# A one-core transformer block: a new instruction order whose model knows that VectorE and GpSimd block each other, layer norm in small groups, reciprocals as Ln and Exp

## The chip, the cores and the metric

The kernel runs on one core of one Trainium2 chip. The metric is the device time of one launch in microseconds (us). The kernel before took 233.0 us (median of 3 runs, 232.33 to 233.59). Its output was right against the reference.

## The reference, cut to what matters

One token block of 2048 rows and 512 columns goes through a modulated layer norm, linear attention with 32 heads, a second modulated layer norm and a gated feed-forward of width 1376. In the attention, queries and keys become features by two softmaxes over 16 values each (of the projection and of its negative).

```python
mod = silu(c) @ w_mod                      # shifts sa, sb; scales ca, cb; gates ga, gb
h = layernorm(x) * (1 + ca) + sa
q, k, v = split(h @ wqkv)                  # 32 heads of 16
phi_q = [softmax(q w_phi), softmax(-q w_phi)]
phi_k = [softmax(k w_phi), softmax(-k w_phi)]
kv = phi_k^T v;  z = sum(phi_k)
o = (phi_q kv) / (phi_q z + 1e-6)
x = x + ga * (o @ wo)
h = layernorm(x) * (1 + cb) + sb
x = x + gb * ((sigmoid(h @ w_gate) * (h @ w_up)) @ w_down)
```

## The kernel before

The kernel is a graph of tasks. Each task has the engines that may do it with a duration for each, a due time and an earliest time. When the kernel is built, a list scheduler plays the graph through and writes every engine's queue in the resulting order. In the traces each engine works its queue in that order, so a task that waits stops everything behind it (run e11 shows it: two sums start only when 12.39 us of scaling ahead of them on GpSimd are done).

```python
# Graph.order(), cut: the ready task with the earliest due time takes the free engine with the shortest duration
engs = [e for e in t.alts if free_at[e] <= now + 1e-9]
...
e = min(engs, key=lambda e: t.alts[e])
```

Sixteen tiles of 128 rows go through the "K stage": layer norm 1, K and V projections (the feature weights are folded into the K and Q weights first), exp, sum, reciprocal, product, and the kv matmuls. Layer norm 1 works in groups of four tiles. The first two groups are transposed on TensorE, the others by DMA:

```python
for g in range(4):
    ...
    def f_rs(e, sl=sl):                                   # rstd of four tiles, on GpSimd
        pool.tensor_scalar(ve1[:, sl], mv1[:, sl, 1], 1e-5, None, op0=ALU.add)
        pool.tensor_tensor(rs1[:, sl], ve1[:, sl], mhalf[:, sl], op=ALU.pow)
    # nmr1 = -mean * rstd, the bias of the normalisation on ScalarE or GpSimd:
    dve.scalar_tensor_tensor(nmr[:, 0, sl], mv1[:, sl, 0], -1.0, rs1[:, sl], ...)
...
G.add(f"e{t}.{a}", {"ACT": 1.12 * w}, f_e, ...)           # exp of k and of -k
G.add(f"n{t}.{a}", {"DVE": 0.08 + 1.13 * w}, f_n, ...)    # ks = sum over 16
G.add(f"r{t}.{a}", {"DVE": 0.06 + 0.5 * w}, lambda e, ...: dve.reciprocal(ks, ks), ...)
G.add(f"phi{t}.{a}", {"POOL": 0.05 + 1.9 * w} ..., f_p)   # phi = e * ks
```

After kv come, in units of one tile and later of two, the division of the attention, the output projection, layer norm 2, and the gate and up matmuls of the feed-forward:

```python
act.copy(smS[:, 0:nt], sm[:, 0:nt, 0:128])                # PSUM to SBUF
def f_small(...):
    dve.tensor_tensor(m[:, 0:nt], smS[:, 0:nt, 0:64], smS[:, 0:nt, 64:128], op=ALU.mult)
    dve.tensor_tensor(den[:, 0:nt], m[:, 0:nt, 0:32], m[:, 0:nt, 32:64], op=ALU.add)
    dve.reciprocal(den[:, 0:nt], den[:, 0:nt])
    dve.tensor_tensor(cc[:, 0:nt], smS[:, 0:nt, 64:128]..., den[:, 0:nt]..., op=ALU.mult)
```

GpSimd also scales wo by ga (4 pieces, shared with VectorE) and wd by gb (11 pieces, "wd scaling"), the latter soon after kv. The silu at the start uses Tanh, as does the sigmoid of the feed-forward.

## Time and profile before

| what | before | how to read it |
|---|---|---|
| time | 233.0 us | median of 3 runs; the profiled run has a span of 230.8 |
| TensorE work at full rate | 197.0 us | worked out in the prediction |
| steady K matmuls from | 15.3 us | what lies before is the start |
| last kv matmul ends | 69.7 us | end of the K stage |
| first gate matmul | 90.2 us | after it TensorE has one hole, of 0.50 us |
| ScalarE busy | 103.1 us (45%) | VectorE 75%, GpSimd 36% |
| table loads on ScalarE | 1 | see below |

The prediction shows the main lines.

A table load is an instruction on ScalarE's own queue of 1.283 us. In the K stage (15.3 to 69.7 us) ScalarE is busy for 42.90 of 54.40 us and VectorE for 49.07.

### The profile page before, as it was taken

The numbers are of one execution on the slowest core, as the hardware profiler recorded it, in microseconds if no ns is written. First come the engines' busy times: TensorE is split into PE (matmuls) and PEld (weight loads), VectorE is DVE, ScalarE is ACT, GpSimd is POOL, SyncE is SP. The second block draws the span as 40 slices with busy tenths as digits, with TensorE's granted clock in tenths as the row PEclk, the third lists the DMA queues.
The fourth block names the chain that finished last, engine by engine and source line by source line (L and its number), as shares of the span: only waits on it lengthen the run. The fifth ranks groups of instructions, "written<-read, shape, count | busy, mean of one in ns | idle before, by whom it ended". The sixth has DMA issues, their size and how long they took to land.

```text
span 230.8 us, 4164 instructions
## 1 busy us (share of the span) xinstructions
PE 206.3 (89%) x1526; PEld 117.6 (51%) x1526; DVE 172.3 (75%) x355; ACT 103.1 (45%) x207; POOL 82.4 (36%) x91
## 2 busy tenths in 40 slices
PE   0588798899889769999999999999999999999990
PEld 0563555355445457876877544445454444444430
DVE  0689998759997998978999974958677988432430
ACT  2578685879785546443453233252321432322100
POOL 6405599679499725323200620110430300000000
PEclk9999999999999967999999999999999999999998
DMA  6974836059900002113222220132202061000011
GB/s 173 366 285 91 313 141 97 0 103 378 341 6 3 0 0 48 24 27 71 45 68 57 46 59 3 26 68 68 48 0 68 0 104 47 12 1 23 27 59 43
DMA packets 30333, 19.27 MB, mean 83 GB/s; under 512 B 22257, under 2 KB 27746, under 8 KB 30306
## 3 DMA queue, kind: packets, MB, share of 16 engines
q1 hardware_dynamic: 30272, 18.91, 29.1%
q8 instruction: 14, 0.23, 0.4%
q0 software_dynamic: 32, 0.02, 0.2%
q14 instruction: 13, 0.11, 0.2%
q10 hardware_dynamic: 2, 0.00, 0.0%
HBM read 11.58 MB, written 2.10 MB: 59 GB/s over the span
## 4 chain that ended last, share of the span: by engine, by line
PE 60%; ACT 0%; DVE 0%; issue 0%
PE u_ps L471 17%; PE g_ps L471 17%; PE y_ps L491 16%; PE a_ps L396 6%; PE num L363 2%; PE sm L338 1%; ACT eT L772 0%; PE q_ps L767 0%; DVE ot L500 0%; PE tp_x L443 0%; PE bnd L526 0%
## 5 line engine op out<-in xcount | busy, mean ns | idle before, releaser
L475 ACT ACTIVATE tg<-g_ps 128x512 bf16<-128x512 f32 (+5 forms) x66 | 29.5, 454 | 70.1 <-PE g_ps L471 59.1
L480 DVE SCALAR_TENSOR_TENSOR wmod_sb<-tg,u_ps 128x512 bf16<-128x512 bf16 (+5 forms) x66 | 32.3, 503 | 25.8 <-PE u_ps L471 21.7
L491 PE MATMUL y_ps<-wd_sb,wmod_sb 128*128 128x512 bf16 (+1 forms) x176 | 44.4, 379 | 0.0
L725 POOL TENSOR_TENSOR phi<-e,ks 128x1024 bf16<-128x1024 bf16 (+1 forms) x15 | 28.3, 1898 | 11.3 <-DVE ks L730 5.0
L471 PEld LDWEIGHTS <-wg_sb 128*128 128x128 bf16 (+1 forms) x264 | 23.5, 100 | 17.3 <-DVE wT_sb L450 0.5
L471 PEld LDWEIGHTS <-wu_sb 128*128 128x128 bf16 (+1 forms) x264 | 23.6, 100 | 16.4 <-issue 0.8
L387 POOL TENSOR_TENSOR o<-u 128x512 bf16<-128x512 f32 x14 | 17.9, 1287 | 35.6 <-DVE u L369 33.9
L471 PE MATMUL g_ps<-wT_sb,wg_sb 128*128 128x512 bf16 (+3 forms) x132 | 27.0, 326 | 0.0
L471 PE MATMUL u_ps<-wT_sb,wu_sb 128*128 128x512 bf16 (+3 forms) x132 | 26.8, 326 | 0.0
L491 PEld LDWEIGHTS <-wmod_sb 128*128 128x128 bf16 (+1 forms) x176 | 16.9, 98 | 17.5
L471 PE MATMUL u_ps<-wqk_sb,wu_sb 128*128 128x128 bf16 (+5 forms) x132 | 22.1, 290 | 0.5 <-ACT eT L772 0.5
L471 PE MATMUL g_ps<-wqk_sb,wg_sb 128*128 128x128 bf16 (+5 forms) x132 | 22.2, 290 | 0.0
L369 DVE TENSOR_TENSOR u<-num,cc 128x512 f32<-128x512 f32 (+1 forms) x32 | 20.6, 679 | 1.2 <-PE num L363 1.1
L722 DVE TENSOR_REDUCE ks<-e 128x64 f32<-128x1024 bf16 (+1 forms) x18 | 19.0, 1064 | 2.2 <-ACT e L719 2.2
L719 ACT ACTIVATE e<-k_ps 128x512 bf16<-128x512 f32 x32 | 17.2, 611 | 5.0 <-PE k_ps L706 3.4
L772 ACT ACTIVATE eT<-q_ps 128x512 bf16<-128x512 f32 x32 | 16.7, 621 | 3.7 <-PE q_ps L767 2.6
L706 PE MATMUL k_ps<-wqk_f,h1T 128*128 128x512 bf16 x64 | 16.2, 380 | 1.5 <-ACT h1T L691 0.8
L396 PE MATMUL a_ps<-wo_sb,oT 128*128 128x512 bf16 x64 | 16.1, 394 | 0.7 <-ACT eT L772 0.7
L412 POOL TENSOR_SCALAR ve<-mv 128x2 f32<-128x2 f32 (+1 forms) x9 | 2.0, 225 | 41.1 <-DVE mv L406 39.9
L710 PE MATMUL v_ps<-wv_sb,h1T 128*128 128x512 bf16 x64 | 16.1, 379 | 0.1
L767 PE MATMUL q_ps<-h1T,wqk_f 128*128 128x512 bf16 x64 | 15.5, 379 | 0.0
L500 DVE TENSOR_TENSOR ot<-y_ps,x 128x512 bf16<-128x512 f32 x16 | 11.0, 686 | 5.9 <-PE y_ps L491 5.8
(110 smaller groups left out, 280.8 us busy)
## 6 DMA issues: line engine op xcount, KB each, us to landing
x_sb<-in_A_x_dram SPq DMA_DIRECT2D x4, 512.0 KB, 9.9
wmod_sb<-in_w_mod_dram SPq DMA_DIRECT2D x1, 2048.0 KB, 8.0
out_dram<-ot SPq DMA_DIRECT2D x16, 128.0 KB, 1.8
wg_sb<-in_B_w_gate_dram SPq DMA_DIRECT2D x1, 1376.0 KB, 7.5
wu_sb<-in_B_w_up_dram SPq DMA_DIRECT2D x1, 1376.0 KB
wd_sb<-in_B_w_down_dram SPq DMA_DIRECT2D x1, 1280.0 KB, 13.5
wqk_sb<-in_A_wqkv_dram SPq DMA_DIRECT2D x2, 512.0 KB, 5.9
wmod_sb<-in_w_mod_dram SPq DMA_DIRECT2D x1, 1024.0 KB, 8.4
```

The costliest lines, as they stand in the source:

```text
L369: dve.tensor_tensor(u[:], ps[:].rearrange("p (h d) -> p h d", d=DH), cc[:, q, s, :].unsqueeze(2).to_broadcast([P, H, DH]), op=ALU.mult)
L387: G.add(f"o{t}", {"POOL": 1.3}, lambda e, ub=ub, o=o: pool.tensor_tensor(o[:], ub[0][:].rearrange("p h d -> p (h d)"), ub[1][:].rearrange( ...
L396: pe.matmul(ap_[:], lhsT=oT[:, j, :], rhs=wo_sb[:, j, :], start=(j == 0), stop=(j == KT - 1))
L471: pe.matmul(ps[:fsz, 0:n], lhsT=w[:, j, ft * P:ft * P + fsz], rhs=h[:, j, 0:n], start=(j == 0), stop=(j == KT - 1))
L475: G.add(f"tg{k}.{ft}", {"ACT": 0.15 + n * 0.00088}, lambda e, tg=tg, g_ps=g_ps, fsz=fsz, n=n: act.activation(tg[:fsz, 0:n], g_ps[:fsz, 0:n ...
L480: dve.scalar_tensor_tensor(hm_all[:fsz, hm[k].slot, ft, 0:n], tg[:fsz, 0:n], 1.0, u_ps[:fsz, 0:n], op0=ALU.add, op1=ALU.mult)
L491: pe.matmul(y[:], lhsT=hm_all[:fsz, hm[k].slot, ft, tl * P:(tl + 1) * P], rhs=wd_sb[:fsz, ft, :], start=(ft == 0), stop=(ft == FT - 1))
L706: pe.matmul(kp[:], lhsT=h1T[:, j, t * P:(t + 1) * P], rhs=wqk_f[:, j, D:2 * D], start=(j == 0), stop=(j == KT - 1))
L719: act.activation(ee[:, s].rearrange("p h j -> p (h j)"), kp[:], ACT.Exp, scale=1.0 - 2.0 * s)
L722: dve.tensor_reduce(ks[:, a:b], ee[:, a:b], axis=AX.X, op=ALU.add)
L725: engine(e).tensor_tensor(ph[:].rearrange("p (s h j) -> p s h j", s=2, j=DH)[:, a:b], ee[:, a:b], ks[:, a:b].unsqueeze(3).to_broadcast([P, ...
L772: act.activation(eT[cq][:, s * 4 + blk, :], qp[:], ACT.Exp, scale=1.0 - 2.0 * s)
```

## The change

Its intent is to take out the places where VectorE and GpSimd block each other and to fill TensorE's holes. By "lock" I mean below what the traces show: beside a GpSimd operation some VectorE operations take several times as long (in the kernel before, den, with two SBUF inputs, took 1.05 us for 128x32 under the wd scaling and 0.22 for 128x64 after it). The scheduler's model gets this lock, better durations and searched due times: in the code, tasks marked with `port` don't run on the two engines at one time. Layer norm 1 works in groups of one and two tiles, all transposed on TensorE. Some of the reciprocals go from VectorE, and some rstd from GpSimd, to ScalarE as exp(-ln x) and exp(-0.5 ln x). Warm-up matmuls are meant to keep TensorE active at the start (e4 shows what they bring). Three groups of queries are held back to fill the gap after kv. The wd scaling comes later, and the small division reads PSUM. The silu's Tanh becomes an Exp, and a tiny Tanh ("tsw") after the last planned Ln/Exp pair is meant to fetch Tanh's table before the gates need it.

```diff
+LG = [[0], [1], [2, 3], [4, 5], ... [14, 15]]            # groups of layer norm 1
+RS1 = [{"ACT": 0.4}] * 3 + [{"POOL": 1.1, "ACT": 0.4}] * 6
+RK = [['DVE'], ['DVE', 'ACT'], ['ACT'], ...]             # who may do the reciprocal of tile t
+WDREL, WDDUE, WDSTEP = 78.45, 153.49, 1.05
 ... # the scheduler
+                if engs and all(e in t.port for e in engs) and port_free > now + 1e-9:
+                    port_wait = True
+                engs = [e for e in engs if e not in t.port or (port_free <= now + 1e-9 and not port_wait)]
 ... # the small division
-                dve.tensor_tensor(m[:, 0:nt], smS[:, 0:nt, 0:64], smS[:, 0:nt, 64:128], op=ALU.mult)
-                dve.tensor_tensor(den[:, 0:nt], m[:, 0:nt, 0:32], m[:, 0:nt, 32:64], op=ALU.add)
+                dve.tensor_tensor(m[:, 0:nt], sm[:, 0:nt, 0:64], smS[:, 0:nt], op=ALU.mult)
+                dve.tensor_reduce(den[:, 0:nt], m[:, 0:nt].rearrange("p q (s h) -> p q h s", h=32), axis=AX.X, op=ALU.add)
 ... # rstd, in layer norm 1; in layer norm 2 for the first unit
+            if e == "ACT":
+                act.activation(ve1[:, sl], mv1[:, sl, 1], ACT.Ln, bias=eps[:, 0:1])
+                act.activation(rs1[:, sl], ve1[:, sl], ACT.Exp, scale=-0.5)
+            else: ... # add and pow on GpSimd, as before
 ... # softmax reciprocal
+                if e == "ACT":
+                    act.activation(ks[:, a:b], ks[:, a:b], ACT.Ln)
+                    act.activation(ks[:, a:b], ks[:, a:b], ACT.Exp, scale=-1.0)
+                else:
+                    dve.reciprocal(ks[:, a:b], ks[:, a:b])
+            rw = {"DVE": 0.06 + 0.5 * w, "ACT": 0.36 + 0.08 * w}
 ... # silu at the start, the tiny Tanh
-    G.add("c2", ..., act.activation(..., ACT.Tanh, scale=0.5), ...)
+    G.add("c2", ..., act.activation(..., ACT.Exp, scale=-1.0), ...)
+                G.add("tsw", {"ACT": 1.5}, lambda e: act.activation(tsw[:], tsw[:], ACT.Tanh), ...)
 ... # scalings
-        G.add(f"wo{j}", {"POOL": 1.2, "DVE": 0.65}, ...)
+        G.add(f"wo{j}", {"POOL": 1.28}, ...)
-              r=[...], w=[("wd", ft)], due=GB + 5.0 + ft, rel=GB - 10.0)
+              r=[...], w=[("wd", ft)], due=WDDUE + WDSTEP * ft, rel=WDREL)
 ... # start: x in smaller loads, 22 warm-up matmuls, w_mod in two halves; transposes of all tiles on TensorE
```

The model counts 0.40 to 0.44 us for a reciprocal on ScalarE and 0.4 for an rstd: two activations.

## The prediction

> **What bounds the kernel now.** I read the page first (engine shares and slices), then the chain that ended last, then busy time in stretches that I chose from TensorE's timeline, then the waits, then the timelines of VectorE and GpSimd where TensorE has holes. From the page, engine shares, the slice rows of TensorE, and the chain by line:
>
> ```profile
> PE 206.3 (89%) x1526; PEld 117.6 (51%) x1526; DVE 172.3 (75%) x355; ACT 103.1 (45%) x207; POOL 82.4 (36%) x91
> ...
> PE   0588798899889769999999999999999999999990
> ...
> PEclk9999999999999967999999999999999999999998
> ...
> PE u_ps L471 17%; PE g_ps L471 17%; PE y_ps L491 16%; PE a_ps L396 6%; PE num L363 2%; PE sm L338 1%; ACT eT L772 0%; PE q_ps L767 0%; DVE ot L500 0%; PE tp_x L443 0%; PE bnd L526 0%
> ```
>
> From slice 16 (92 us) to the last, TensorE has no hole, and the chain is TensorE alone. The time is therefore TensorE's work, plus what it lost before 92 us, plus a tail. The stretches (busy us and count of PE, PEld, DVE, ACT, POOL; clock; DMA share; GB/s):
>
> ```profile
> 15.30:69.70 54.40, 48.41 (x360) 26.31 (x361) 49.07 (x76) 42.90 (x82) 40.40 (x29) 1.00 0.54 159
> 69.70:90.20 20.50, 17.40 (x176) 11.29 (x174) 18.27 (x37) 10.50 (x23) 13.25 (x13) 0.83 0.04 8
> 90.20:224.50 134.30, 133.76 (x911) 73.86 (x909) 96.76 (x222) 42.33 (x88) 22.53 (x28) 1.00 0.18 41
> ```
>
> "Busy" flatters TensorE, so I count its work at the start-to-start spacing of its dense stretches: 0.216 us for 512 columns (four in 0.86), 0.108 for 256, 0.056 for 128, 0.059 for the kv matmuls (eight in 0.47), 0.025 for the narrow ones (32 in 0.80). With the counts of the groups: 440 wide ones (K, V, Q, out, y, the two gate vectors) 95.0; gate and up 9.8 + 9.5 + 57.0; num 7.3; kv 7.6; sm 3.2; modulation 1.6; transposes and fold 6.1. Sum 197.0 us. The last y ends at 224.5, the tail from there to the end is 6.3 (one VectorE add, the store, the closing branch). So TensorE lost 224.5 - 197.0 = **27.5 us**:
> - 11.5 until the K matmuls run steadily at 15.3 (3.8 us of work in it);
> - 8.2 from there to the last kv at 69.7 (54.4 less 46.2 of work: K 13.6, V 13.8, kv 7.6, eight of the 16 query blocks 6.9, the rest 4.3);
> - 7.1 from 69.7 to 92.2 (22.5 less 15.4), where the first gate matmul is at 90.2;
> - 0.7 after it.
>
> The holes have two causes. [...] In the middle, VectorE and GpSimd are in each other's way. VectorE's timeline, start, length, operation, in the attention head of the first one-tile unit and of a later two-tile unit:
>
> ```profile
> 72.10 0.63 DVE L348 TENSOR_TENSOR m<-smS 128x64 f32<-128x64 f32 x1 [0.77 <-ACT smS L342]
> 72.76 1.05 DVE L349 TENSOR_TENSOR den<-m 128x32 f32<-128x32 f32 x1
> ...
> 79.36 0.28 DVE L348 TENSOR_TENSOR m<-smS 128x128 f32<-128x128 f32 x1
> 79.67 0.22 DVE L349 TENSOR_TENSOR den<-m 128x64 f32<-128x64 f32 x1
> ```
>
> Half the elements took two to five times as long. What differs is GpSimd, in its own timeline:
>
> ```profile
> 65.66 13.70 POOL L756 TENSOR_TENSOR wd_sb<-wd_sb,wmod_sb 128x512 bf16<-128x512 bf16 x11
> ```
>
> The same shows on VectorE's wo scaling (4.36 us for three, at 54.6, under two phi on GpSimd), which then left GpSimd idle for 3.04 us for want of ks, and so kv and its matmuls waiting.
>
> [...] the first transposes start about 0.1 us apart (16 in 1.6 to 1.7 us) against 0.056 later, and the granted clock is 0.71 in 80 to 86 us, after a hole of 1.9 us. [...] The one load of this trace took 1.28 us.
>
> **The change, part by part.**
>
> *TensorE's work.* Layer norm 1 of tiles 8 to 15 goes from DMA transposes to TensorE: 32 more transposes x 0.056 = +1.8 us. All other real work stays: 198.8 us. The 22 warm-up matmuls are meant for the idle start and cost the end nothing if they stay there.
>
> *Start.* x comes in two tiles (256 KB) rather than four, ahead of wk. Between x and wk, 512 KB took 2.0 us (5.2 to 7.2), so wk lands about 1.0 us earlier, at 6.2. Transposes and fold at 0.056 rather than 0.104 save 32 x 0.048 = 1.5 us, the copies of wT on two engines about 0.6 more; K waits for one tile's layer norm and not four (12 fewer transposes, and h1T pieces of 0.2 to 0.4 instead of 0.5 to 0.75). The other path, the modulation, ends the earlier half: its load (1 MB) was in at 10.1, now at about 9.1, plus two 0.4 us pieces of which one is done before, plus copies 0.35. I take steady K from 11.8, with 3.0 us of work before it: **loss 8.8** (was 11.5).
>
> *K stage.* VectorE's load between 12 and 70 us falls: wo on GpSimd (-4.4), phi of the last tiles on GpSimd (-4.0), about half of the 16 reciprocals of 0.55 to ScalarE (-4.4), xn partly moved (8 x 0.60 before, about -2), nmr and lock waits (-1); added are h1T writes (about 20 x 0.33 against 3.8 us, +2.8), copies and a memset (+1.4). That is -11.6 us of 49. GpSimd: 16 phi x 1.95 = 31.2, four wo 5.1, some xn 4 and rs 3: 43 us, against 40.4 before, but with less idling. ScalarE: exps 17.2, V copies 9.3, half of the reciprocals 3, LN pieces 8, one or two query groups of 5 each. So all three stand near 45 us where 48 are available, and TensorE's own 47 us (K, V, kv, the transposes, fold, one to two query groups) become the bound. Steady K at 11.8 and the last kv at 60 to 62 instead of 69.7. It will not fit perfectly: **loss 3.0** (was 8.2).
>
> *From kv to the first gate.* The wd scaling (13.7 us) is released only from 78 us of the model, den becomes a reduction, m and cc read PSUM: the two first units lose their lock waits, about 1.0 + 0.8 us of the 2.8 us chain, so some 1.8 each and 3.6 in series. The first rstd goes to ScalarE (0.4 for GpSimd's 0.24 + 0.59). A table switch (1.28) to Tanh sits beside the modulation, partly hidden. The chain of 20.5 becomes 15 to 16; held-back queries (three groups, 10.4 us of TensorE work, though 1.1 us per block on ScalarE) fill most of it, which also holds the clock. **Loss 3.0** (was 7.1). First gate at 76 to 77 instead of 90.
>
> *After that* TensorE stays full as now: **0.6**.
>
> Sum: 198.8 + 8.8 + 3.0 + 3.0 + 0.6 + 6.3 = 220.5 us of span. The timed runs lie about 2 us over the span (233.0 and 232.5 against 230.8): **222.5 us**, 4.5% faster.
>
> **Rivals.**
> - *The order is the model's, not the chip's.* Queues run in order, and tuned due times (offsets like 24.54) fit a model; each misjudged duration stops whatever stands behind. For it: the order before is a model's too, with K stage planned at 2.45 us a tile and taken at 3.4 (54.4 / 16). Against: the new model knows the lock, the largest error seen. If half of the gains in the K stage and the chain go, that is 4.7 us back: 227.
> - *ScalarE becomes the bound.* It gains reciprocals as two activations each, table loads and later query exps. Were each Ln/Exp pair to reload a table (some 20 x 1.28 us) it would cost over 20 us and the time would go to 240. Against: [...] an explicit switch to Tanh is placed once. With 45% busy now it has room; I think 5% of this.
> - *The late wd scaling collides in the dense stretch:* 11 x 1.28 us on GpSimd next to 14 o sums of 1.29, and locks against VectorE's modulation. y waits for wd piece by piece. 134 us with GpSimd at 22.5 has room; at worst 2 us: 224.5.
> - *The plan fully met:* loss after the start about 2 instead of 6.6: 218.
>
> **Range and chances.** The start is nearly certain to give 2 to 3 us, the lock in the chain 3 more, less 1.8 of new transposes; that alone reaches 228 to 229. The K stage decides the rest. 217 to 228.5 should hold it 8 times in 10. Faster than 228.3 (2%): 0.87; within: 0.11; slower: 0.02.
>
> **What would show it.** Steady K matmuls from about 12 us, starting transposes 0.06 us apart; last kv near 61; den pieces of the first units at 0.2 to 0.4 us; no row with 1.5 us for a scaling of wo on VectorE; first gate near 76; two or three table loads; granted clock near 1 between 60 and 80; no hole after the first gate. Wrong if kv still ends after 66 (then look for what ScalarE or GpSimd waits for), if holes appear among the gates (late wd, or exps of held-back queries), or if table loads number in the tens.

The 3 us for half of the reciprocals on ScalarE and the 5% of the second rival rested on something: I took it that Ln and Exp would share one load, which no trace had shown. The trace of the kernel before shows that TensorE waits 4.53 us for the load of wqk, to 7.21 us, and that its first 16 transposes then take 1.89 us from the first start to the last end. "Holds the clock" goes by two of the stretches: the granted clock was 0.83 where TensorE was busy for 17.40 of 20.50 us, and 1.00 where it was busy for 133.76 of 134.30.

## More of the kernel before

From the page, ScalarE's row of busy tenths in 40 slices:

```profile
ACT  2578685879785546443453233252321432322100
```

and from its groups of instructions (line, engine, operation, count, then total busy us and mean ns of one, then idle time before it and what ended that):

```profile
L570 ACT ACT_TABLE_LOAD x1 | 1.3, 1283 | 1.3 <-PEq L863 1.3
```

No instruction in the text of either kernel loads a table, and the trace of the kernel before has one load: they are put in on the way to the chip.

## The result, and the profile after

The changed kernel took **249.13 us** (median of 4 runs, 248.93 to 249.66) beside 232.73 for the kernel before (4 runs): 7.0% slower. A ratio here is the mean time of one kernel's fast runs over that of the other's of the same rounds, so it is not quite the ratio of the medians; it is 1.0703, with a 95% interval of 1.0666 to 1.0739. The profiled run has a span of 247.4 us.

From the page: engine shares, four rows of slices, and the chain that ended last, by engine and by line.

```profile
PE 219.6 (89%) x1580; PEld 123.0 (50%) x1580; DVE 163.6 (66%) x366; ACT 134.0 (54%) x255; POOL 87.1 (35%) x100
...
PE   7497968748499899999999999999999999999990
...
ACT  3979997799959968975335222162210540312000
...
PEclk9959998797689999999999999999999999999997
...
PE 67%; ACT 17%; DVE 6%; issue 4%; POOL 2%; DMA 1%; DVEq 0%; POOLq 0%; ACTq 0%
PE y_ps L543 16%; PE g_ps L523 15%; PE u_ps L523 15%; PE a_ps L441 5%; PE num L408 3%; PE v_ps L782 3%; PE q_ps L846 2%; DVE ks L794 2%; PE k_ps L778 2%; ACT L805 2%; ACT L727 2%; ACT e L791 2%; PE kvacc L323 2%; ACT L728 2%; ACT L804 2%
```

ScalarE has 31 us more work than before (134.0 against 103.1), although the two-instruction reciprocals themselves are small. In the first 16 slices its row stands at 9 again and again where it mostly stood at 5 to 8, and TensorE's row has 4s in the K stage with a lower clock after them (0.75 granted in 44 to 69 us). And the chain, which was TensorE alone in the prediction's lines, is now to 17% ScalarE, on four lines without an output name. The groups of instructions tell what those are:

```profile
L727 ACT ACT_TABLE_LOAD x5 | 6.4, 1283 | 0.9 <-DVE sc L624 0.8
L728 ACT ACT_TABLE_LOAD x5 | 6.4, 1283 | 0.1
L804 ACT ACT_TABLE_LOAD x5 | 6.4, 1283 | 0.1
L805 ACT ACT_TABLE_LOAD x5 | 6.4, 1283 | 0.1
L628 ACT ACT_TABLE_LOAD x1 | 1.3, 1283 | 1.3 <-PEq L942 1.3
L458 ACT ACT_TABLE_LOAD x1 | 1.3, 1283 | 0.0
L459 ACT ACT_TABLE_LOAD x1 | 1.3, 1283 | 0.0
```

Lines 727 and 804 are the two Ln, 728 and 805 their Exp (458 and 459 are the pair of layer norm 2, 628 the first Exp of the kernel). Eleven pairs, 22 loads, and one at the start: 23 x 1.283 = 29.5 us of ScalarE. In order of time, on ScalarE (start, length, line, operation):

```profile
49.59 1.28 ACT L727 ACT_TABLE_LOAD   x1
50.88 0.30 ACT L727 ACTIVATE ve<-mv,eps 128x2 f32<-128x2 f32 x1
51.19 1.28 ACT L728 ACT_TABLE_LOAD   x1
52.49 0.20 ACT L728 ACTIVATE rs<-ve 128x2 f32<-128x2 f32 x1
52.71 1.28 ACT L804 ACT_TABLE_LOAD   x1
54.00 0.26 ACT L804 ACTIVATE ks<-ks 128x64 f32<-128x64 f32 x1
54.28 1.28 ACT L805 ACT_TABLE_LOAD   x1
55.57 0.26 ACT L805 ACTIVATE ks<-ks 128x64 f32<-128x64 f32 x1
55.73 0.57 ACT L813 CAST vaug<-v_ps 128x512 bf16<-128x512 f32 x1
```

Every Ln fetches a table and every Exp after it fetches another. The second load starts 1.60 us after the first (49.59 to 51.19), 1.28 for the load and 0.30 for the Ln. Two pairs cost 6.14 us (49.59 to 55.73), of which 1.02 is calculation. Behind them in the queue stands the V copy, and TensorE waits for it. TensorE's own timeline (in brackets: idle before it, and what ended that):

```profile
12.71 0.61 PE L757 MATMUL tp_h<-ident,xn 128*128 128x128 bf16 x4 [3.94 <-ACT xn L743]
56.35 0.27 PE L757 MATMUL tp_h<-ident,xn 128*128 128x128 bf16 x2 [4.40 <-ACT vaug L813]
65.47 0.37 PE L757 MATMUL tp_h<-ident,xn 128*128 128x128 bf16 x2 [3.44 <-ACT e L791]
106.81 0.39 PE L523 MATMUL g_ps<-wqk_sb,wg_sb 128*128 128x128 bf16 x4
```

The three holes of 3.4 to 4.4 us each follow a run of loads, and the first gate matmul, at 90.2 before, starts at 106.81. The stretches that answer to the prediction's (K stage, from kv to the first gate, the dense rest; busy us and count of PE, PEld, DVE, ACT, POOL, then the clock, DMA share and GB/s):

```profile
17.78:88.81 71.03, 55.62 (x385) 30.92 (x384) 42.78 (x85) 62.90 (x110) 41.07 (x35) 0.87 0.31 105
88.81:106.81 18.00, 17.91 (x183) 10.65 (x181) 16.53 (x44) 15.82 (x35) 10.43 (x11) 1.00 0.08 16
106.81:241.10 134.29, 133.60 (x919) 74.26 (x917) 96.49 (x216) 42.88 (x92) 31.16 (x35) 1.00 0.18 40
```

The last two stretches are full. Nearly all the loss lies at the start and in the K stage, where ScalarE is busy for 62.90 of 71.03 us while VectorE and GpSimd, meant to be the tight ones, have room. I count the loss as the prediction does: the time of a stretch less TensorE's work at full rate. With 198.8 us of work in all (3.15 before the first steady V matmul, 45.2 in the K stage, 17.7 from kv to the first gate, the rest after it) the loss is 14.6 + 25.8 + 0.3 + 1.5 = 42.2 us, against 27.5 before.

The intended effects are there too. VectorE's small division in the first unit after the change, which the prediction showed at 0.63 and 1.05 us before:

```profile
91.17 0.23 DVE L393 TENSOR_TENSOR m<-sm,smS 128x64 f32<-128x64 f32 x1 [0.71 <-ACT smS L387]
91.43 0.22 DVE L394 TENSOR_REDUCE den<-m 128x32 f32<-128x64 f32 x1
```

### The profile page after: what moved, and what is told of

The parts are those of the page before. It is cut to its first block, busy times and chain, and to the rows that moved or that the text cites. A ratio compares the mean times of both kernels' runs of the same rounds, so it can differ in the third digit from the quotient of the medians.

```text
span 247.4 us, 4314 instructions
## 1 busy us (share of the span) xinstructions
PE 219.6 (89%) x1580; PEld 123.0 (50%) x1580; DVE 163.6 (66%) x366; ACT 134.0 (54%) x255; POOL 87.1 (35%) x100
## 4 chain that ended last, share of the span: by engine, by line
PE 67%; ACT 17%; DVE 6%; issue 4%; POOL 2%; DMA 1%; DVEq 0%; POOLq 0%; ACTq 0%
PE y_ps L543 16%; PE g_ps L523 15%; PE u_ps L523 15%; PE a_ps L441 5%; PE num L408 3%; PE v_ps L782 3%; PE q_ps L846 2%; DVE ks L794 2%; PE k_ps L778 2%; ACT L805 2%; ACT L727 2%; ACT e L791 2%; PE kvacc L323 2%; ACT L728 2%; ACT L804 2%
## 5 line engine op out<-in xcount | busy, mean ns | idle before, releaser
L543 PE MATMUL y_ps<-wd_sb,wmod_sb 128*128 128x512 bf16 (+1 forms) x176 | 45.7, 379 | 0.2 <-ACT tg L527 0.2
L797 POOL TENSOR_TENSOR phi<-e,ks 128x1024 bf16<-128x1024 bf16 (+1 forms) x18 | 31.0, 1734 | 23.8 <-issue 8.6
L523 PE MATMUL u_ps<-wqk_sb,wu_sb 128*128 128x128 bf16 (+3 forms) x176 | 31.1, 299 | 0.5 <-DVE wmod_sb L532 0.5
L523 PE MATMUL g_ps<-wqk_sb,wg_sb 128*128 128x128 bf16 (+3 forms) x176 | 31.1, 299 | 0.0
L757 PE MATMUL tp_h<-ident,xn 128*128 128x128 bf16 x64 | 7.9, 238 | 18.0 <-ACT xn L743 6.3
L782 PE MATMUL v_ps<-wv_sb,h1T 128*128 128x512 bf16 x64 | 20.1, 450 | 0.5 <-DVE h1T L762 0.5
L778 PE MATMUL k_ps<-wqk_f,h1T 128*128 128x512 bf16 x64 | 18.0, 410 | 0.2 <-ACT h1T L764 0.2
L523 PE MATMUL u_ps<-wT_sb,wu_sb 128*128 128x256 bf16 (+3 forms) x88 | 17.9, 326 | 0.0
L523 PE MATMUL g_ps<-wT_sb,wg_sb 128*128 128x256 bf16 (+3 forms) x88 | 17.9, 326 | 0.0
L441 PE MATMUL a_ps<-wo_sb,oT 128*128 128x512 bf16 x64 | 15.4, 379 | 0.1
L757 PEld LDWEIGHTS <-xn 128*128 128x128 bf16 x64 | 5.0, 106 | 21.3 <-issue 12.4
```

The lines of the kernel that those rows point to most:

```text
L441: pe.matmul(ap_[:], lhsT=oT[:, j, :], rhs=wo_sb[:, j, :], start=(j == 0), stop=(j == KT - 1))
L523: pe.matmul(ps[:fsz, 0:n], lhsT=w[:, j, ft * P:ft * P + fsz], rhs=h[:, j, 0:n], start=(j == 0), stop=(j == KT - 1))
L543: pe.matmul(y[:], lhsT=hm_all[:fsz, hm[k].slot, ft, tl * P:(tl + 1) * P], rhs=wd_sb[:fsz, ft, :], start=(ft == 0), stop=(ft == FT - 1))
L778: pe.matmul(kp[:], lhsT=h1T[:, j, t * P:(t + 1) * P], rhs=wqk_f[:, j, D:2 * D], start=(j == 0), stop=(j == KT - 1))
L782: pe.matmul(vp[:], lhsT=h1T[:, j, t * P:(t + 1) * P], rhs=wv_sb[:, j, :], start=(j == 0), stop=(j == KT - 1))
L797: engine(e).tensor_tensor(ph[:].rearrange("p (s h j) -> p s h j", s=2, j=DH)[:, a:b], ee[:, a:b], ks[:, a:b].unsqueeze(3).to_broadcast([P, ...
```

## The experiments

Theory A: the table loads are the whole loss, and without them the change is worth what it was made for. Rivals: the small activations on a full ScalarE, whatever the loads, are the cost; or the order itself is bad (the prediction's first rival). Twelve kernels were run in three calls; each call has its own runs of the kernel before (7 each, medians 232.36, 233.0 and 232.16). Each kernel ran 4 times. All outputs are right. Differences between kernels are of medians; across calls they are good to about 1 us, and where that matters the difference by the ratios is given too.

| kernel | edit in short | us | ratio to before (95%) |
|---|---|---|---|
| e1_oneset | changed kernel, one table for Ln and Exp | 226.47 | 0.9762 (0.9721 to 0.9802) |
| e2_rs_reloads | e1, loads back at 5 rstd | 235.35 | 1.0142 (1.0101 to 1.0183) |
| e3_r_reloads | e1, loads back at 5 reciprocals | 234.03 | 1.0059 (1.0006 to 1.0112) |
| e4_nowarm | e1 without warm-up matmuls | 228.04 | 0.9836 (0.9787 to 0.9884) |
| e5_noln | changed kernel without Ln, re-ordered | 241.1 | 1.0338 (1.0299 to 1.0378) |
| e6_nmr | e1, nmr with a pointer operand | 223.27 | 0.9601 (0.9565 to 0.9638) |
| e7_oldlock | e1, old small division and early wd | 236.48 | 1.0144 (1.0109 to 1.0179) |
| e8_before_lock | kernel before, lock remedies alone | 233.75 | 1.0023 (0.9989 to 1.0057) |
| e9_noln_kept | e1's order, Ln/Exp replaced in place | 232.01 | 1.0005 (0.9954 to 1.0056) |
| e10_noln_kept_nmr | e9 with e6's nmr | 228.4 | 0.9861 (0.98 to 0.9922) |
| e11_wd_early | e1, early wd only | 229.14 | 0.987 (0.9832 to 0.9909) |
| e12_oldform | e1, old small division only | 231.06 | 0.9968 (0.9913 to 1.0023) |

### e1_oneset: one load serves Ln and Exp

```diff
+    def table(i):
+        nc.add_instruction(mybir.InstLoadActFuncSet(..., engine=Activation, act_func_set_id=i))
+    def f_c2(e):
+        table(6)                                   # one load for both Ln and Exp
+        act.activation(c_ps[:, KT:2 * KT], c_ps[:, 0:KT], ACT.Exp, scale=-1.0)
```

The order of all other instructions is that of the changed kernel. With this load in place none is put in before a Ln or an Exp: from 4 to 90 us, with all eleven pairs, e1's trace has one load, and that stands before the Tanh.

> The changed kernel, with one line more: the table set that holds both Ln and Exp is loaded by hand before the first activation. Every engine's order stays as it is, only table loads go: 23 in the changed kernel, 2 here (one at the start, one at the switch to Tanh). Theory A (the reloads made it slower, the rest of the prediction holds): 21 x 1.28 = 27 us less of ScalarE work, nearly all ahead of the first gate; time 219 to 228 us, faster than the kernel before by 2% or more. Rival B (the order is the model's and does not fit the chip): only what lay openly on the path comes back, holes of TensorE remain in the K stage, time above 233 us, no better than before. Rival C (TensorE's extra transposes and clock): time near 240.

Measured: 226.47 us (226.41 to 226.96), 22.7 us below the changed kernel (for 21 loads less, 1.08 us a load) and 2.4% below the kernel before. Its row of the clock, and the stretches between the same matmuls as above:

```profile
PEclk9999969999999999999999999999999999999996
```

```profile
12.62:65.98 53.36, 48.75 (x385) 28.39 (x384) 45.41 (x87) 42.81 (x94) 40.97 (x35) 0.97 0.47 163
65.98:83.67 17.69, 17.69 (x183) 10.62 (x181) 16.21 (x43) 15.29 (x34) 10.10 (x11) 1.00 0.08 16
```

The same 385 matmuls of the K stage take 53.36 instead of 71.03 us: 17.7 us. The start is 5.16 us shorter (12.62 against 17.78), about the 4 loads that stood before it (4 x 1.283 = 5.13). In e2 below, where those four loads are back, it is 4.35 us longer than in e1. From kv to the first gate at most 0.3 us is lost in either. Two loads are left: the one placed by hand, and one of 1.28 us at 77.25, before the tiny Tanh, so what was loaded by hand didn't serve that function. So the loads are the loss, and theory A holds, but for one point: the interval of the ratio ends at 0.9802, so "2% or more" below the kernel before is likely and not certain.

### e2_rs_reloads and e3_r_reloads: the loads back, one kind at a time

```diff
+                table(5)                           # e2: rstd of layer norm 1; e3: the softmax reciprocal
                 act.activation(..., ACT.Ln, ...)
+                table(6)
                 act.activation(..., ACT.Exp, ...)
```

> As e1_oneset, but the five Ln/Exp pairs of layer norm 1 load a table before each half again (10 loads, 12.8 us, most of them before 25 us and two pairs at 50 to 65). Order unchanged. Theory A: these sit in the chain that starts the first tiles, so 7 to 13 us over e1_oneset. Rival B (loads mostly hidden in ScalarE's slack): under 4 us over e1_oneset.

> As e1_oneset, but the five Ln/Exp reciprocals of the softmax load a table before each half again (10 loads, 12.8 us, spread over the K stage). Order unchanged. Theory A: ScalarE is the busiest engine there, so 6 to 13 us over e1_oneset; and the gaps of e2 and e3 together give 80% or more of the gap between the changed kernel and e1_oneset. Rival B: under 4 us over e1_oneset.

Measured: 235.35 and 234.03 us, that is 8.9 and 7.6 us over e1 for ten loads of 1.283 us each. Both kinds cost about 0.8 to 0.9 us a load. Together they give back 16.5 of the 22.7 us (73%); I had expected at least 80%. Besides these twenty the changed kernel has layer norm 2's two loads (and not e1's one for Tanh); they cost at most the 0.3 us by which its stretch from kv to the gate differs. The rest must come from the two kinds together costing more than their sum: in the K stage e2 and e3 lose 4.5 and 7.4 us over e1, and both together lose 17.7. The traces split these 5.8 us. In the K stage TensorE is idle for 4.6 us in e1, 7.2 in e2, 9.7 in e3 and 15.4 in the changed kernel, and its matmuls are busy for 48.8, 50.7, 51.0 and 55.6 us, at a granted clock of 0.97, 0.93, 0.94 and 0.87. So 3.1 us are more holes, and 2.7 us are slower matmuls. Why the holes add up to more than their sum stays open. That ScalarE has no slack left isn't enough: it is busy for 91% of the K stage in e3 already, and for 89% in the changed kernel.

### e4_nowarm: without warm-up matmuls

```diff
-            for _ in range(n):
+            for _ in range(0):
                 pe.matmul(ps[:], lhsT=wd_sb[:, FT - 1, 0:P], ...)
```

> As e1_oneset, but the 22 warm-up matmuls are not issued (order of the rest unchanged). If warm-up is worth what I predicted, the first transposes are about 0.1 us apart instead of 0.056 and the time is 1 to 2.5 us over e1_oneset. Rival: the modulation and its load set the start, and the difference is under 0.7 us.

Measured: 228.04, 1.6 us over e1. TensorE's first 16 transposes of the weights, with them in e1 and without them here:

```profile
7.14 1.06 PE L686 MATMUL tp_w<-ident,wqk_sb 128*128 128x128 bf16 x16
```

```profile
7.64 1.89 PE L686 MATMUL tp_w<-ident,wqk_sb 128*128 128x128 bf16 x16 [4.96 <-DMA wqk_sb<-in_A_wqkv_dram]
```

Sixteen transposes take 1.06 instead of 1.89 us after an idle start. Warm-up is a small, real part of the change.

### e5_noln: no Ln at all, and a new order

```diff
+RK = [['DVE']] * 16
+RS1 = [{"POOL": 1.1}] * 9
-            G.add(f"rs2_{p}", {"ACT": 0.4} if first and p == 0 else {"POOL": 0.64 + 0.18 * nt}, ...)
+            G.add(f"rs2_{p}", {"POOL": 0.64 + 0.18 * nt}, ...)
```

> The changed kernel with everything but the Ln/Exp: all reciprocals on VectorE, all rstd on GpSimd, no table set by hand, the scheduler orders anew; one table load. Theory A (reloads are the whole of the loss, the other parts gain): clearly faster than the kernel before, 225 to 231 us. If Ln/Exp in one set is itself worth something (11 x 0.5 us off VectorE, GpSimd's start at 0.4 instead of 1.1), it is 1 to 4 us over e1_oneset's 226.5. Rival: the gain of e1_oneset hangs on Ln/Exp, and this is within 1% of the kernel before (230 to 235).

Measured: 241.1, a clear miss, although this kernel has a single load. The stretch from about the last kv (which ends at 65.4) to the first gate, and that gate in TensorE's timeline:

```profile
66.00:98.50 32.50, 21.89 (x242) 14.01 (x241) 30.49 (x64) 16.24 (x36) 24.27 (x25) 0.87 0.12 25
```

```profile
98.52 0.59 PE L525 MATMUL g_ps<-wT_sb,wg_sb 128*128 128x128 bf16 x4 [4.27 <-DVE u L416]
```

The K stage is as short as e1's, but 33 us lie between the last kv and the first gate, with VectorE busy 30.49 of 32.5. The scheduler, given other alternatives under due times searched for the old ones, put VectorE's division of later tiles and the modulation of a later chunk (3.98 us at 93.89) ahead of what the first gates wait for. This confounds two things, the Ln and the order, so e9 keeps the order. What e5 shows already: with an order of its own the K stage needs no Ln to end as early (65.4, and 65.98 in e1).

### e6_nmr: the bias of the normalisation without a second SBUF input

```diff
-dve.scalar_tensor_tensor(nmr[:, 0, sl], mv1[:, sl, 0], -1.0, rs1[:, sl], op0=ALU.mult, op1=ALU.mult)
+[dve.tensor_scalar(nmr[:, 0, t:t+1], mv1[:, t, 0:1], rs1[:, t:t+1], -1.0, op0=ALU.mult, op1=ALU.mult) for t in ts]
 # the same for layer norm 2; starts from e1, order unchanged
```

In e1 the nmr operation of two times two numbers per partition sometimes took over 1 us. VectorE's timeline of e1 (two of them), with what GpSimd does in the second case:

```profile
33.36 0.15 DVE L742 SCALAR_TENSOR_TENSOR nmr<-mv,rs 128x2 f32<-128x2 f32 x1
...
40.51 1.61 DVE L742 SCALAR_TENSOR_TENSOR nmr<-mv,rs 128x2 f32<-128x2 f32 x1
```

```profile
40.18 1.93 POOL L804 TENSOR_TENSOR phi<-e,ks 128x1024 bf16<-128x1024 bf16 x1 [0.78 <-POOL xn L754]
```

The long one ends at 42.12, with phi at 42.11; the two others, of 1.09 and 1.15 us, end within 0.02 us of a phi as well. So a tiny operation waits for the end of a long one: the lock that the prediction spoke of, on an operation that the change's own model left at 0.16 us.

> e1_oneset with the -mean*rstd product as one tensor_scalar a tile (one SBUF tensor and a scalar operand a partition) instead of a scalar_tensor_tensor of two SBUF tensors; order unchanged. In e1_oneset three of those took 1.09, 1.15 and 1.61 us on VectorE under a phi on GpSimd, against 0.10 to 0.15 alone. Theory L (the lock still eats the K stage): they fall to 0.25 us a pair, K stage 2 to 4 us shorter, 223 to 225 us. Rival (something else waits there, or a tensor_scalar locks as well): within 0.7 us of e1_oneset.

Measured: 223.27 us (222.53 to 224.47), 4.0% below the kernel before and the best. The groups of this operation in layer norm 1, in e1 and in e6:

```profile
L742 DVE SCALAR_TENSOR_TENSOR nmr<-mv,rs 128x2 f32<-128x2 f32 x7 | 4.4, 627 | 0.0
```

```profile
L742 DVE TENSOR_SCALAR nmr<-mv,rs 128x1 f32<-128x1 f32 x16 | 2.4, 189 | 0.0
```

and e6's row of the clock, and its K stage:

```profile
PEclk9999999999999999999999999999999999999999
```

```profile
11.89:62.81 50.92, 46.84 (x386) 27.16 (x384) 43.89 (x94) 42.62 (x95) 40.98 (x35) 1.00 0.51 174
```

The K stage is 2.4 us shorter than e1's, though the operation itself only saves 2.3 us of VectorE in layer norm 1. None of the 16 new operations took more than 0.206 us, though GpSimd is busy for 40.98 of the 50.92 us and pairs of them ran under a phi (at 23.54, 25.48, 38.67 and 42.70): none of them waited. A hole of 1.28 us in e1 (to 29.80) is gone, and so are the slow matmuls after it (four of V in 1.70 us, from 31.03, against 0.86 in e6; the granted clock in 28 to 34 us was 0.72 in e1 and 1.00 in e6). 0.28 of these 6 us is about 1.7 us, an estimate from the two clocks, so a good part of the 2.4 may be the clock. Of the 3.8 us of span, 0.7 are the earlier start, and that may be chance: kernels with the same start began V between 11.89 and 12.97.

### e7_oldlock, e11_wd_early, e12_oldform: what the lock remedies after kv are worth

```diff
 # e12: the small division as before (two SBUF inputs, tensor_tensor for den), nothing else
 # e11: the wd scaling's times as before, nothing else:
-        ..., due=WDDUE + WDSTEP * ft, rel=WDREL)
+        ..., due=GB + 5.0 + ft, rel=GB - 10.0)
 # e7: both; all start from e1
```

> e1_oneset with m, den and cc in the old form (two SBUF inputs each) and the wd scaling due as early as before (11 in a row, ahead of the first o). If the lock waits of the chain from kv to the first gate are worth what I predicted (3.6 us): m and den of the first units take 0.6 and 1.05 us again, first gate 3 to 4 us later, time 2 to 5 us over e1_oneset. Rival: the held-back queries fill the longer chain and the time is under 1 us over it.

> e1_oneset with the wd scaling due early (11 in a row on GpSimd before the first o), m, den and cc left in the new form; orders on VectorE follow. e7_oldlock had both and lost 10 us. If the lock is the cost (old form under wd), this keeps den at 0.22 to 0.3 us and loses under 3 us. If the early wd and the order that follows from it are the cost (first o and rstd wait behind 12.5 us of wd), it loses 5 to 10 us.

> e1_oneset with m, den and cc in the old form, wd late as in the changed kernel, order unchanged. Only the four wo scalings (4.5 us from 65.6) lie beside the first unit, so at most its m and den are locked: 0 to 2 us over e1_oneset. If it loses 4 us or more, the old form alone is the cost of e7_oldlock.

Measured: e7 236.48, e11 229.14 and e12 231.06, which is 10.0, 2.7 and 4.6 us over e1 by the medians, and 8.9, 2.5 and 4.8 by the ratios (their difference times 232.5). I had expected 2 to 5 for e7 and 0 to 2 for e12; e11 is under the 3 us that its text gives to the lock as the cause. VectorE's timeline in e7, first unit and the two-tile unit that comes third:

```profile
69.33 0.67 DVE L397 TENSOR_TENSOR m<-smS 128x64 f32<-128x64 f32 x1 [0.77 <-ACT smS L391]
70.03 1.05 DVE L398 TENSOR_TENSOR den<-m 128x32 f32<-128x32 f32 x1
...
76.64 1.26 DVE L397 TENSOR_TENSOR m<-smS 128x128 f32<-128x128 f32 x1
```

The first two run under the wo scaling on GpSimd (66.50 to 71.04), the third under wd, and all are locked. Three units stand ahead of the second tile's u, not two. From the first m to that u VectorE takes 10.8 us (69.33 to 80.11) against 4.9 in e1 (68.34 to 73.25): 5.9 us for the lock. With wd early but the new forms (e11) the lock doesn't show (den took 0.22 us in the first unit, under wo, and in the second, under wd), and the cost is that GpSimd's queue runs in order; there, in e11:

```profile
69.69 12.39 POOL L842 TENSOR_TENSOR wd_sb<-wd_sb,wmod_sb 128x512 bf16<-128x512 bf16 x11
82.05 2.49 POOL L436 TENSOR_TENSOR o<-u 128x512 bf16<-128x512 f32 x2
```

In e1 the same two o sums start at 77.33, after 7.24 us of idling. With the old forms alone (e12) the first unit is still locked, by the wo scaling (65.88 to 70.40), the next two are clear, and the lock comes back when the late wd scaling starts beside a later unit:

```profile
69.40 1.05 DVE L398 TENSOR_TENSOR den<-m 128x32 f32<-128x32 f32 x1
...
83.89 1.25 DVE L397 TENSOR_TENSOR m<-smS 128x128 f32<-128x128 f32 x1
```

```profile
87.73 0.47 PE L527 MATMUL g_ps<-wqk_sb,wg_sb 128*128 128x128 bf16 x3 [2.38 <-DVE wqk_sb L506]
```

TensorE waits 2.38 us in the middle of the first gate group and then runs at about half rate until 92 (four matmuls of the gates in 0.43 us from 88.87, against 0.22 later in e11; granted clock 0.63 from 87.5). So neither half of the remedy is enough by itself: late wd moves the collision, and the new forms make it harmless. The forms are the larger part (4.6 us without them, 2.7 without the late wd). Together they are worth 9 to 10 us, of which the two alone explain 7.3.

### e8_before_lock: the lock remedies in the kernel before

```diff
 # small division from PSUM with tensor_reduce, as in the change; wo on GpSimd alone; and
-        ..., due=GB + 5.0 + ft, rel=GB - 10.0)
+        ..., due=GB + 30.0 + ft, rel=GB + 10.0)
```

> The kernel before with only the changes against the lock: m and cc read PSUM, den is a tensor_reduce, wo is scaled on GpSimd alone, wd released 20 us later in the model. If these alone carry a good part of the gain of e1_oneset: 228 to 231 us against 232.4, first gate 2 to 4 us earlier than 90.2. Rival (they pay only along with the early start and the held-back queries): within 1 us of the kernel before.

Measured: 233.75, the same as before (1.0023). The remedy works where it is applied: the den pieces of the first units take 0.22 us and the first gate starts at 84.56 instead of 90.2. But those 5.6 us are given back. (The profiled run is the slowest of the four, 235.41, so its waits may be longer than usual.) TensorE's waits (total, times, longest):

```profile
PE y_ps L491 <- DVE wmod_sb L480: 1.9, 1, 1.9
PE a_ps L396 <- DMA oT<-o: 1.8, 1, 1.8
PE g_ps L471 <- DVE wT_sb L450: 1.6, 1, 1.6
```

None of the three stands in the list of the kernel before. The likely reading, which no run tests, is that the order behind the chain was made for the late gate, and that with an early one the next tiles aren't ready. Much the same remedy is worth 9 to 10 us in an order made for it and nothing in this one. Which of its parts brings each of these waits, I did not separate.

### e9_noln_kept and e10_noln_kept_nmr: the Ln/Exp pairs replaced in place

```diff
-                if e == "ACT":
-                    act.activation(ks[:, a:b], ks[:, a:b], ACT.Ln)
-                    act.activation(ks[:, a:b], ks[:, a:b], ACT.Exp, scale=-1.0)
-                else:
-                    dve.reciprocal(ks[:, a:b], ks[:, a:b])
+                dve.reciprocal(ks[:, a:b], ks[:, a:b])
 # likewise rstd: add and pow on GpSimd. Every queue otherwise keeps e1's order; no load placed by hand
```

> e1_oneset with every engine's order kept, but each Ln/Exp pair replaced where it stands: the reciprocals by VectorE's reciprocal, the rstd by GpSimd's add and pow; one table load. e5_noln did the same but let the scheduler order anew and took 241.1. Theory O (e5 lost by its order after kv, not by missing Ln/Exp: its kv ended at 65.4, e1_oneset's at 66.0): first gate near 84, time 225 to 229 us. Theory N (Ln/Exp are needed): above 232 us.

> e9_noln_kept with the mean*rstd product of e6_nmr. If the lock gain of e6 (3.2 us) does not depend on Ln/Exp: 2 to 4 us under e9_noln_kept, and about e6_nmr's 223.3 plus what e9 shows over e1_oneset. If Ln/Exp matter once the locks are gone: 2 us or more over e6_nmr.

Measured: e9 232.01, 5.5 us over e1 (5.7 by the ratios). That is outside theory O's 225 to 229 and at the very edge of theory N's "above 232"; the first gate is at 89.7, not near 84. Theory O was right on one point: from kv to the gate e9 takes 17.7 us (72.0 to 89.7) without any Ln, so e5's 33 us there were its order. The loss of e9 lies before that; e10 228.4, 3.6 under e9. Steady V starts at 14.90 in e9 (12.62 in e1), because the first two rstd now stand on GpSimd behind another task: its rstd operations, 0.23 and 0.58 us, run from 8.6 to 10.3, where e1's activations were through by 6.8. The K stage takes 57.1 us (14.90 to 72.0) against 53.4. So moving these operations to ScalarE is worth some 5 us at this order, if they cost no loads; e5, with kv done at 65.4 in an order of its own, suggests that this is not what Ln/Exp are worth in themselves. And e6's step gains as much without any Ln in the kernel (3.6 us, and 3.2 or by the ratios 3.7 with it): the two are independent as far as these pairs show.

## Why the prediction was wrong, point by point

**The step that failed** is an assumption: that Ln and Exp would share one load. On it the change's part on the K stage took 3 us for half of the reciprocals, and the second rival got 5%. It was mine, and no trace had shown it. One load can serve both, as e1 shows with one for eleven pairs. But nothing in the changed kernel asks for it, and its trace has a load before every Ln and another before every Exp after it, 22 for the eleven pairs. I took what one load can serve for what would be loaded. The rival described exactly this, "Were each Ln/Exp pair to reload a table (some 20 x 1.28 us) it would cost over 20 us and the time would go to 240", and the page of the kernel before couldn't refute it: there was no Ln in it. The loads cost 22.7 us (e1), and the time went to 249, further than the rival's 240, since the rest of the change also brought 4 us less than planned.

**The sum, with the loads and without**, loss in us by stretch:

| stretch | before | predicted | changed | e1 | e6 |
|---|---|---|---|---|---|
| start | 11.5 | 8.8 | 14.6 | 9.5 | 8.7 |
| K stage | 8.2 | 3.0 | 25.8 | 8.2 | 5.7 |
| kv to the first gate | 7.1 | 3.0 | 0.3 | 0 | 0 |
| after it | 0.7 | 0.6 | 1.5 | 1.9 | 1.3 |
| sum | 27.5 | 15.4 | 42.2 | 19.6 | 15.7 |

**TensorE's work.** 198.8 us held: 1580 matmuls, that is 32 transposes and 22 warm-ups over the 1526 before, and the stretch from kv to the gate takes 17.69 us, all of it busy.

**Start.** Right without the loads: 9.5 in e1 and 8.7 in e6 for 8.8. In the changed kernel four loads at 5.2 to 11.7 us held up the first normalised tile, which is the hole of 3.94 us.

**K stage.** Mis-sized even without the loads: 8.2, not 3.0. It lost the same as before, with 45.2 us of work in it (46.2 before). The term that failed is VectorE's: the prediction took 11.6 us off its 49, and in e1 it is busy for 45.41, 3.7 us less. (Its own sum, 37, doesn't fit its "near 45" either.) The largest miss is nmr, which was booked as a gain ("nmr and lock waits (-1)"): it went from 1.2 us to 4.4, since smaller groups mean more such operations (9 in layer norm 1 against 2), each of which can land under a phi (three of e1's did, at 1.09 to 1.61 us). Besides, 13 of the 18 reciprocal instructions stayed on VectorE, not about half, and the statistics of 13 tiles instead of 10 fell into the stage (11.2 us against 8.4). Without the nmr lock 5.7 us of loss remain (e6).

**From kv to the gate.** Better than predicted: nothing is lost, for 3.0 predicted. The size of the lock was right: from the first m to the second tile's u VectorE takes 8.63 us in the kernel before (72.10 to 80.73) and 4.90 in the changed one (91.17 to 96.07), 3.7 us for my 3.6. In e7 the lock hits three units and costs 5.9. But my stretch of 15 to 16 us with a loss of 3.0 had room for only 12 to 13 us of work, and TensorE has 17.7 there, 9.5 of them held-back queries. So it is longer than I said, and full; and the first gate comes later than my 76 to 77 (83.67 in e1, 80.50 in e6), for this and because kv ends at 65.98 and 62.81, not near 61. Work done before the gate isn't lost.

**Late wd in the dense stretch.** The loss after the gate rose from 0.7 to 1.5 us (1.9 in e1), within the third rival's 2 and over my 0.6; what of it is wd I did not separate. e12 shows that the collision is there if the forms are old.

**"The order is the model's, not the chip's."** The changed order, made with no loads for Ln and Exp in its model, gains 6 us as soon as the chip makes none for them either. The rival was right in another sense: the model's 0.4 us for a pair, where the chip took 3.1, is what sank it. And e5 and e8 show how brittle such an order is.

**Range.** 217 to 228.5 holds e1 and e6, not the kernel that was asked about. The 2% that I gave to "slower" was the real error: one assumption that no line of the trace supported carried 20 us, and 5% was too little for it.

## What to carry to other kernels

Before moving work to ScalarE with a new function, count the table loads in a trace, and don't assume that two functions share one: an Ln/Exp pair cost 0.5 us with a shared table and 3.1 without, and one load placed by hand before the first activation turned a 7% loss into a 2.4% gain. Look at the tiniest VectorE operations when GpSimd is busy: one with two SBUF inputs can wait for the end of a GpSimd instruction (up to 1.61 us for 128x2 numbers here), and a form with a per-partition pointer operand cured it here (0.189 us in the mean of 16) for another 1.6 points (e6, 223.3 us, is the version to keep). And judge a remedy in the order it will run in: much the same lock remedies were worth about 9 us in one order and nothing in the other.
